# Moving the copies of x from ScalarE to VectorE in the first batch row of an attention and mixer kernel, and one load to another queue

## The chip, the cores and the metric

The kernel runs on one core of a Trainium2 chip. The metric is device time in microseconds (us), the median of a few executions. The core has four engines that compute: TensorE (PE; PEld is its weight load), VectorE (DVE), ScalarE (ACT) and GpSimd (POOL). SyncE (SP) only issues transfers, and ScalarE can issue them too. Each engine works through its own list of instructions in order. When the next instruction waits for data or for a free buffer, everything behind it on that engine waits as well, so the order of a list matters as much as its length.

## The reference

Eight batch rows of eight heads of thresholded attention are followed by a mixer: an MLP over tokens and an MLP over channels, both with a residual. Everything is float32.

```python
# q, k, v: (8, 8, 576, 64)
scores = scale * q @ k^T
thresh = max(scores, axis=-1) - tau
scores = where(scores >= thresh, scores, -1e9)
attn   = exp(scores - max(scores));  attn = attn / (sum(attn) + 1e-9)
x      = (attn @ v) laid out as (8, 576, 512)
# mixer
h   = relu(x^T @ w_tok1) @ w_tok2;   u = x + h^T
out = u + relu(u @ w_ch1) @ w_ch2
```

The four weight matrices arrive as 64-bit floats. The kernel converts them to 32-bit floats on the chip, in pieces, while it works.

## The kernel before

The work goes in units: 18 per batch row, 128 query rows of one pair of heads each (two of the 18 are shared by two pairs). Unit u has these stages: TensorE makes the scores; VectorE takes the row maxima (`mx`); ScalarE applies the threshold and the exponential (`e`, with row sums `rs`); VectorE inverts the sums (`rr`); GpSimd scales `e`. Two units later TensorE turns `e` (128x128 transposes into PSUM) and the turned blocks are copied to SBUF (`eT`). One unit after a group is complete TensorE multiplies it with the values (`pv` in PSUM), and that result is copied to SBUF as a part of `x` (kept transposed, `xT`). The turned blocks and `pv` share a pool of two PSUM buffers.

```python
ps_tr = ctx.enter_context(tc.tile_pool(name="ps_tr", bufs=2, space=bass.MemoryType.PSUM))
...
def scores(u):
    ...                                   # 8 or 16 matmuls into sc[0], sc[1]
    for h in range(2):
        nc.vector.tensor_reduce(out=mx[:, c], in_=sc[h][:, :, 0:HS], axis=AX.XY, op=ALU.max)
        nc.gpsimd.tensor_scalar(out=bias[:, c], in0=mx[:, c], ...)
def norm(u):
    nc.vector.tensor_scalar(out=rr, in0=rs, ...)
    nc.vector.reciprocal(out=rr, in_=rr)
    ...                                   # 2x nc.gpsimd.tensor_scalar: e times rr
def turn(u, third):
    ps = ps_tr.tile(...)                  # 3 transposes of 128x128 into ps
    on = nc.scalar.copy if third == 1 and u % 2 else nc.vector.tensor_copy
    on(out=eT[...], in_=ps)               # 128x384
def values(b, p, c):
    ps = ps_tr.tile(...)                  # 20 matmuls into ps
    ...
    nc.scalar.copy(out=x, in_=ps)         # 128x256, or 128x64 for a shared unit
```

From the second batch row on `e` is turned in another way: by a 32x32 transpose on VectorE and by transfers (`turn_blocks`).

A piece of weights is converted in three steps (k is the number of the step). `weight_to` issues steps up to a number, and each step gives work to several engines:

```python
def weight(n):
    for k in range(steps_done, ...):
        i, part = divmod(k, 3)
        if part == 0:
            on_gpsimd(i - 1)              # one add on GpSimd; then the raw buffer is free
            if i: load_piece(i - 1 + NRAW)
        else:
            on_scalar(i + 1, part - 1)    # ScalarE prepares the next piece
        on_vector(i, part)                # part 0: tensor_scalar; 1 and 2: scalar_tensor_tensor
```

The main loop, cut to what concerns the first batch row (`b_now` is 0 in units 0 to 17):

```python
for u in range(len(units) + LAG + 4):
    if on: scores(u)
    if due and not in_blocks(due[0][1]):
        values_due(u)                     # pv and its copy on ScalarE
    if 0 < u <= len(units): norm(u - 1)
    if b_now: weight(2)
    if back:
        for i in range(3): turn(w, i)     # w = u - 2, first batch row only
        ...
    if b_now: weight(2)
    else:     weight_to(2.25 * (u - 1.5)) # first step(s) of the unit
    if on: weigh(u)                       # threshold and exponential on ScalarE
    ...
    else:     weight_to(2.25 * (u - 1))   # second step(s) of the unit
    ...                                   # loads; prep(): VectorE transposes q and k of a pair
```

At the start the loads are issued in this order: q and k of pair 0 (on SP and ACT), weight piece 0 (SP), q and k of pair 1 (on SP and ACT), piece 1, v of pair 0, pieces 2 and 3, v of pair 1.

Of the kernel before, what the change touches and what calls it, by code (L numbers as in the profile page):

```python
# [21 lines left out]
def kernel(  # L22
# [26 lines left out]
    nc = tc.nc  # L49
# [47 lines left out]
    def load_qk(n, eng, part=None):  # L97


        b, p = pairs[n]  # L100
        if n not in loaded:
            loaded[n] = [ld.tile([P, S // 32, 32], F32, tag=tag, name=f"{tag}_{n}") for tag in ("lq", "lk")]
        for i in range(4) if part is None else (part,):
            h, c = divmod(i, 2)
            for src, t, on in zip((q, k), loaded[n], eng):
                on.dma_start(
                    out=t[32 * i : 32 * i + 32], in_=src[b, 2 * p + h, :, 32 * c : 32 * c + 32].rearrange("(n t) d -> t n d", t=32)
                )
# [29 lines left out]
    NRAW = 4  # L138
    raw_at = [scratch[:, 2 * WMAX * i : 2 * WMAX * (i + 1)] for i in range(NRAW)]

    def like(x, dst):
        if len(dst.shape) == 2:
            return x
        return x.rearrange("p (a b) -> p a b", a=dst.shape[1])
# [22 lines left out]
    def load_piece(i):  # L167
        if i >= len(pieces):
            return
        dst, src = pieces[i]  # L170
        rows = dst.shape[0]
        n = 1
        for d in dst.shape[1:]:
            n *= d
        raw = raw_at[i % NRAW][0:rows, 0 : n * (2 if wide(i) else 1)].bitcast(src.dtype)
        nc.sync.dma_start(out=like(raw, dst), in_=src)
        if wide(i):
            words = raw.bitcast(U32).rearrange("p (n w) -> p n w", w=2)
            h2 = work.tile([P, WMAX], F32, tag="o", name=f"h2_{i}")[0:rows, 0:n]
            raws[i] = like(words[:, :, 0], dst), like(words[:, :, 1], dst), like(h2, dst)  # L180
        else:
            raws[i] = like(raw, dst)

    def wide(i):
        return i < len(pieces) and pieces[i][1].dtype == I64

    def on_scalar(i, part):
        if wide(i):
            lo, hi, h2 = raws[i]
            if part == 0:  # L190
                nc.scalar.activation(out=lo.bitcast(I32), in_=lo, func=AF.Copy, scale=2.0**-29)
            else:
                nc.scalar.activation(out=h2, in_=hi.bitcast(F32), func=AF.Square)
# [17 lines left out]
    def on_gpsimd(i):  # L211
        if i >= 0:
            dst = pieces[i][0]
            if wide(i):
                nc.gpsimd.tensor_tensor(out=dst.bitcast(I32), in0=dst.bitcast(I32), in1=raws.pop(i)[0].bitcast(I32), op=ALU.add)
            else:
                nc.gpsimd.tensor_copy(out=dst, in_=raws.pop(i))
# [5 lines left out]
    def weight(n):  # L223

        nonlocal steps_done
        for k in range(steps_done, min(steps_done + n, 3 * len(pieces) + 1)):
            i, part = divmod(k, 3)
            if part == 0:
                on_gpsimd(i - 1)
                if i:  # L230
                    load_piece(i - 1 + NRAW)
            else:
                on_scalar(i + 1, part - 1)
            on_vector(i, part)
            steps_done = k + 1

    def weight_to(x):

        weight(max(int(x) - steps_done, 0))
# [3 lines left out]
        weight(3 * i + 4 - steps_done)  # L243

    load_piece(0)
    load_qk(1, (nc.sync, nc.scalar))
    load_piece(1)
    load_v(0)
    for i in range(2, NRAW):
        load_piece(i)  # L250
    load_v(1)

# [25 lines left out]
    def in_blocks(b):  # L278
        return b > 0
# [105 lines left out]
    def split_middle(n):  # L385
# [4 lines left out]
            nc.gpsimd.tensor_copy(out=vl[r, r], in_=lv[r, NI, :])  # L390
        vals[n] = lv, vl

    def values(b, p, c):

        lv, vl = vals[b * NP + p]
        if b not in xTs:
            xTs[b] = xTs[b + 1] = work.tile([P, NP, 2 * S], F32, tag="xT", name=f"xT_{b}")
        key = (b, p - p % 2, c) if c == "s" else (b, p, c)
        n, N, tok = (1, LAST, MAIN) if c == "s" else (2, 2 * P, 2 * P * c)
        first = LAST * (p % 2) if c == "s" else 0  # L400
        eT = eTs[key] if c == "s" else eTs.pop(key)
        if in_blocks(b):
            eT = eT[:, 0 : NK * n * P].rearrange("p (i c x) -> p c i x", i=4, c=NK)
            eT = eT[:, :, first // 32 : first // 32 + N // (32 * n), :]
        else:
            eT = eT[:, 0 : NK * n * P].rearrange("p (c x) -> p c x", c=NK)[:, :, first : first + N]
        ps = ps_tr.tile([P, MAIN], F32, tag="tr", name=f"pv_{b}_{p}_{c}")[:, 0:N]
        to = ps.rearrange("p (i x) -> p i x", x=32 * n) if in_blocks(b) else ps
        for h in range(2):
            r = slice(D * h, D * h + D)  # L410
            nc.tensor.matmul(to[r], lhsT=vl[:, r], rhs=eT[:, NI], start=True, stop=False, skip_group_check=True)  # L411
        for c in range(NI):
            for h in range(2):
                r = slice(D * h, D * h + D)
                j = (NI + 1) * h + c
                nc.tensor.matmul(to[r], lhsT=lv[:, j, :], rhs=eT[:, j], start=False, stop=(c == NI - 1), skip_group_check=True)  # L416
        x = xTs[b][:, p, S * (b % 2) + tok : S * (b % 2) + tok + N]
        if in_blocks(b) and n == 2:
            x = x.rearrange("p (n i x) -> p i n x", n=n, x=32)
            ps = ps.rearrange("p (i n x) -> p i n x", n=n, x=32)  # L420
        nc.scalar.copy(out=x, in_=ps)  # L421


    def token_mlp(b):
# [93 lines left out]
    def push(b):  # L518
        nonlocal quota
        uT = xTs[b]  # L520
        steps, old = token_mlp(b), list(todo)
        todo.clear()

        for i, step in enumerate(steps):
            n = 2 if i in (NT, NT + NTK) else 1
            todo.extend(old[:n] + [step])
            del old[:n]
        todo.extend(old)
        for i in range(2) if b % 2 == 0 else range(2, (2 * S + GR - 1) // GR):
            todo.extend(channel_mlp(b - b % 2, uT, i))  # L530
        quota = (sum(c for c, _ in todo) - (KEEP if b else KEEP_FIRST)) / (UB - 1)
# [6 lines left out]
    def values_due(u):  # L538
        while due and due[0][0] <= u:
            _, b, p, c = due.popleft()  # L540
            values(b, p, c)
            if p == NP - 1 and c == 1:
                push(b)

    for u in range(len(units) + LAG + 4):
        on = u < len(units)
        if u == UB:
            late.close()
            ps_mm = ctx.enter_context(tc.tile_pool(name="ps_mm", bufs=2, space=bass.MemoryType.PSUM))
        if on:  # L550
            b_now, p0, t = units[u]
            n = b_now * NP + p0
        w = u - LAG
        back = 0 <= w < len(units)
        if on:
            scores(u)

        if due and not in_blocks(due[0][1]):
            values_due(u)
        if 0 < u <= len(units):  # L560
            norm(u - 1)
        if b_now:
            weight(2)
        if back:
            key, place, many = group_of(w)
            if not in_blocks(key[0]):
                for i in range(3):
                    turn(w, i)
            if place == many - 1:
                b, p, c = key  # L570
                if c == 0 and p % 2 == 0:
                    split_middle(b * NP + p)
                if c == "s":
                    split_middle(b * NP + p + 1)
                when = u + (2 if in_blocks(b) else 1)
                due += [(when, b, p + i, c) for i in range(2 if c == "s" else 1)]
        if b_now:
            fill(0.4)
        if back and in_blocks(key[0]):
            turn_blocks(w)  # L580

        if b_now:
            weight(2)
        else:
            weight_to(2.25 * (u - 1.5))
        if on:
            weigh(u)
        elif b_now:
            fill(0.6)
        if b_now:  # L590
            weight(2)
        elif u == 0:
            on_scalar(0, 0)
            on_scalar(0, 1)
        else:
            weight_to(2.25 * (u - 1))
        if on:
            m = n + 2 + t // 4
            if t < 8 and m < len(pairs):
                load_qk(m, (nc.scalar if b_now else nc.sync,) * 2, t % 4)  # L600
                if t % 4 == 3:
                    load_v(m)
            if t == 2:
                prep(n + 1)
            if t == 7 and n + 2 < len(pairs):
                prep(n + 2)
        if due and in_blocks(due[0][1]):
            values_due(u)
# [31 lines left out]
```

## Time and profile before

| | |
|---|---|
| time, median of 3 | 1381.45 us (1379.32 to 1382.13) |
| span of the profiled execution | 1381.3 us |
| busy share of the span | PE 96%, DVE 43%, ACT 43%, POOL 26% |
| copies of x on ScalarE (all batch rows) | 64 of 128x256, 372 ns each |
| first batch row | about 12 to 106 us of the span |

In the views of the profile "busy" is the time in which an engine executed something; a bracket such as `[0.94 <-PE tr L360]` behind an instruction is the idle time just ahead of it on its engine, and what ended it. `L309` is line 309 of the kernel before: L286 are VectorE's transposes of q and k, L304 the score matmuls, L309 the maxima, L319 and L326 the threshold and exponential, L333 and L334 the inverse of the sums, L337 GpSimd's scaling, L360 the turns on TensorE, L362 the copies of turns, L411 and L416 the matmuls with the values, L421 the copies of x, and L201, L205 and L209 VectorE's three conversion steps (L191 and L193 ScalarE's, L215 GpSimd's).

### The profile page before, as it was taken

How to read it: one execution, taken by the hardware profiler on the slowest of the kernel's cores; microseconds unless marked ns; L12 is line 12 of the kernel's file. 1: busy time of each engine (PE TensorE's matmuls, PEld its weight loads, DVE VectorE, ACT ScalarE, POOL GpSimd, SP SyncE). 2: the span in 40 equal slices, each digit the busy share in tenths (PEclk: the TensorE clock that was granted, in tenths of full speed). 3: DMA queues.
4: the chain of work that ended last, by engine and by line, in shares of the span. 5: the costliest groups of instructions: out<-in, count | busy, mean ns of one | idle time of the engine just before them, and what ended most of it. 6: DMA issues, size and time to landing. Idle time of an engine off the chain costs nothing.

```text
span 1381.3 us, 19492 instructions
## 1 busy us (share of the span) xinstructions
PE 1330.3 (96%) x6866; PEld 834.1 (60%) x6866; DVE 590.3 (43%) x1009; ACT 589.5 (43%) x1328; POOL 354.8 (26%) x683
## 2 busy tenths in 40 slices
PE   6887789999999999999999999999999999999998
PEld 3544555646565666665766567565657566575675
DVE  5889875354444443434244444433343453201000
ACT  5776654445445444443434444353434454120110
POOL 3556653232323222222222222221221232100000
PEclk9988999999999999999999999999999999999999
DMA  5444654453444444433433444443333433300000
GB/s 118 109 105 120 180 150 119 109 129 89 110 121 105 98 110 101 105 81 88 109 87 93 104 95 107 99 102 81 94 90 92 110 74 88 83 8 16 8 8 23
DMA packets 257376, 128.34 MB, mean 93 GB/s; under 512 B 208064, under 2 KB 221376, under 8 KB 257280
## 3 DMA queue, kind: packets, MB, share of 16 engines
q1 hardware_dynamic: 129264, 111.16, 30.6%
q10 hardware_dynamic: 128016, 15.94, 7.3%
q8 instruction: 55, 0.90, 0.3%
q14 instruction: 41, 0.34, 0.1%
HBM read 43.25 MB, written 9.44 MB: 38 GB/s over the span
## 4 chain that ended last, share of the span: by engine, by line
PE 88%; DVE 6%; DMA 2%; SPq 1%; issue 1%; ACT 1%; POOL 1%; ACTq 0%; DVEq 0%; POOLq 0%
PE c L487 27%; PE c L471 27%; PE sc L304 11%; PE pv L416 8%; PE t L442 4%; PE t L449 4%; PE pv L411 3%; DVE mx L309 2%; PE c L483 1%; PE tx L433 1%; SPq L381 1%; PE pv_s L416 1%; DVE eT L362 1%; PE tr L360 1%; DMA eT<-T 1%
## 5 line engine op out<-in xcount | busy, mean ns | idle before, releaser
L309 DVE TENSOR_REDUCE mx<-sc 128x1 f32<-128x576 f32 x288 | 204.6, 751 | 488.6 <-PE sc L304 488.6
L471 PE MATMUL c<-xT,wc 128*128 128x256 f32 (+1 forms) x1920 | 401.0, 363 | 6.2 <-ACT g L472 5.0
L487 PE MATMUL c<-wc,g 128*128 128x512 f32 x864 | 390.7, 597 | 0.0
L471 PEld LDWEIGHTS c<-xT,wc 128*128 128x128 f32 x1920 | 335.0, 191 | 76.5 <-issue 29.0
L310 POOL TENSOR_SCALAR bias<-mx,toff 128x1 f32<-128x1 f32 x288 | 79.2, 275 | 803.1 <-DVE mx L309 746.5
L487 PEld LDWEIGHTS c<-wc,g 128*128 128x128 f32 x864 | 157.4, 190 | 175.6 <-issue 173.6
L319 ACT ACTIVATE e<-sc,bias 128x576 f32<-128x576 f32 x288 | 198.8, 739 | 141.4 <-POOL bias L310 141.2
L472 ACT ACTIVATE g<-c 128x256 f32<-128x256 f32 (+1 forms) x240 | 86.9, 362 | 328.8 <-PE c L471 315.4
L337 POOL TENSOR_SCALAR e<-e,rr 128x576 f32<-128x576 f32 x288 | 217.2, 767 | 16.8 <-DVE rr L334 4.7
L326 ACT ACTIVATE e<-e,ntau 128x576 f32<-128x576 f32 x288 | 220.8, 771 | 0.0
L304 PE MATMUL sc<-kT,qT 64*128 64x288 f32 (+1 forms) x1280 | 196.5, 441 | 15.0 <-DVE kT L286 9.7
L371 DVE STREAM_TRANSPOSE T<-e 128x1152 f32<-128x1152 f32 x126 | 172.6, 1370 | 13.3 <-DMA eT<-T 8.5
L304 PEld LDWEIGHTS sc<-kT,qT 64*128 64x128 f32 (+1 forms) x1280 | 107.3, 181 | 91.8 <-issue 44.8
L416 PE MATMUL pv<-eT,lv 128*64 128x256 f32 x1024 | 124.9, 386 | 0.0
L492 DVE COPY o<-c 128x512 f32<-128x512 f32 x36 | 24.9, 692 | 174.5 <-PE c L487 174.5
L416 PEld LDWEIGHTS pv<-eT,lv 128*64 128x64 f32 x1024 | 75.9, 140 | 39.0 <-issue 3.6
L421 ACT COPY xT<-pv 128x256 f32<-128x256 f32 x64 | 23.8, 372 | 174.8 <-PE pv L416 167.0
L449 PE MATMUL t<-w,a 128*128 128x288 f32 x256 | 75.2, 421 | 6.3 <-DVE xT L453 4.3
L442 PE MATMUL t<-x_sb,w 128*128 128x512 f32 x160 | 72.1, 597 | 0.0
L449 PEld LDWEIGHTS t<-w,a 128*128 128x128 f32 x256 | 46.0, 192 | 31.3 <-issue 11.5
L453 DVE TENSOR_TENSOR xT<-xT,t 128x288 f32<-128x288 f32 x64 | 28.2, 446 | 78.1 <-PE t L449 77.4
L326 ACT ACTIVATION_READ_ACCUMULATOR e<-e,ntau 128x1 f32 x288 | 56.6, 196 | 0.0
(48 smaller groups left out, 604.3 us busy)
## 6 DMA issues: line engine op xcount, KB each, us to landing
eT<-T SPq DMA_DIRECT2D x896, 72.0 KB, 2.0
scratch<-in_moe_w_ch_dram SPq DMA_DIRECT2D x24, 512.0 KB, 3.7
lv<-in_v_dram SPq DMA_DIRECT2D x32, 288.0 KB, 3.4
out_dram<-o SPq DMA_DIRECT2D x36, 256.0 KB, 2.1
lk<-in_k_dram ACTq DMA_DIRECT2D x112, 72.0 KB, 2.7
eT<-T SPq DMA_DIRECT2D x224, 36.0 KB, 1.9
lq<-in_q_dram ACTq DMA_DIRECT2D x104, 72.0 KB, 2.2
lq<-in_q_dram SPq DMA_DIRECT2D x24, 72.0 KB, 3.4
```

What stands on the lines that cost most here:

```text
L304: nc.tensor.matmul(sc[h][rows, f, 0:HS], lhsT=qT[r, cols], rhs=kT[r, HS * f : HS * f + HS], start=True, stop=True)
L309: nc.vector.tensor_reduce(out=mx[:, c], in_=sc[h][:, :, 0:HS], axis=AX.XY, op=ALU.max)
L319: nc.scalar.activation(out=eh, in_=sc[h][:, :, 0:HS], func=AF.Prelu, bias=bias[:, h : h + 1], scale=SCALE, alpha=STEEP)
L326: nc.scalar.activation(out=eh, in_=eh, func=AF.Exp, bias=ntau, accum_out=rs[:, h : h + 1])
L337: nc.gpsimd.tensor_scalar(out=eh, in0=eh, scalar1=rr[:, h : h + 1], scalar2=1.0, op0=ALU.mult, op1=ALU.mult)
L371: nc.vector.transpose(out=T.rearrange("p (a c n x) -> p c a n x", a=4, c=NK, n=n)[:, :, :, place, :], in_=e.rearrange("p (c a x) -> p c a ...
L416: nc.tensor.matmul(to[r], lhsT=lv[:, j, :], rhs=eT[:, j], start=False, stop=(c == NI - 1), skip_group_check=True)
L442: nc.tensor.matmul(ps, lhsT=w1[:, t, P * m : P * m + P], rhs=x_sb[:, t, :], start=(t == 0), stop=(t == NT - 1))
L449: nc.tensor.matmul(ps, lhsT=s["a"][:, m, P * c : P * c + P], rhs=w2[:, m, HS * f : HS * f + HS], start=(m == 0), stop=(m == NTK - 1))
L471: nc.tensor.matmul(ps, lhsT=wc1[:, j, c, :], rhs=uT[:, c, GR * i : GR * i + n], start=(c == 0), stop=(c == NCC - 1))
L472: nc.scalar.activation(out=s["g"][:, j, 0:n], in_=ps, func=AF.Relu)
L487: nc.tensor.matmul(flat, lhsT=s["g"][:, j, P * t : P * t + P], rhs=wc2[:, j, :], start=False, stop=(j == NJ - 1), skip_group_check=True)
```

## The change

In the first batch row the copies of `pv` into x go from ScalarE to VectorE. They are not issued where the matmuls are, but held back until after the maxima, the inverse of the sums and the first conversion steps of the unit; the copies of the turned blocks follow them. To have the first conversion steps there, `weight_to(2.25 * (u - 1.5))` moves from behind the turns to ahead of them. The step that hands a finished batch row to the mixer (`push`) waits for the held copies. At the start SP issues the keys of pair 1, which ScalarE issued before, and piece 1 of the weights comes after the values of pair 0. The change is meant to take ScalarE out of a wait for TensorE, and to give VectorE something to do while it waits for the turns. From the second batch row on, the copies of x stay on ScalarE.

```diff
     load_piece(0)
-    load_qk(1, (nc.sync, nc.scalar))
-    load_piece(1)
+    load_qk(1, (nc.sync, nc.sync))
     load_v(0)
-    for i in range(2, NRAW):
+    for i in range(1, NRAW):
         load_piece(i)
     load_v(1)
...
+    copies = deque()
     def values(b, p, c):
...
-        nc.scalar.copy(out=x, in_=ps)
+        if in_blocks(b):
+            nc.scalar.copy(out=x, in_=ps)
+        else:
+            copies.append(lambda: nc.vector.tensor_copy(out=x, in_=ps))
...
             if p == NP - 1 and c == 1:
+                if not in_blocks(b):
+                    return True
                 push(b)
+        return False
...
+        last = False
         if due and not in_blocks(due[0][1]):
-            values_due(u)
+            last = values_due(u)
         if 0 < u <= len(units):
             norm(u - 1)
         if b_now:
             weight(2)
+        else:
+            weight_to(2.25 * (u - 1.5))
+        while copies:
+            copies.popleft()()
+        if last:
+            push(0)
         if back:
...
         if b_now:
             weight(2)
-        else:
-            weight_to(2.25 * (u - 1.5))
         if on:
             weigh(u)
```

## The prediction

> **What bounds the kernel now.** I read the page first (busy shares, then the 40 slices), then the busy time by 20 us, then the waits and the engines' own timelines within the first batch row.
>
> ```profile
> PE 1330.3 (96%) x6866; PEld 834.1 (60%) x6866; DVE 590.3 (43%) x1009; ACT 589.5 (43%) x1328; POOL 354.8 (26%) x683
> ...
> PE   6887789999999999999999999999999999999998
> ...
> DVE  5889875354444443434244444433343453201000
> ```
>
> TensorE is the bound of the whole, but not in the first four or five slices of 34.5 us: there VectorE is at 8 to 9 tenths and TensorE at 6 to 8. The change touches only that stretch.
>
> ```profile
> 40.00:60.00 20.00, 17.03 (x144) 11.03 (x140) 17.04 (x38) 14.79 (x35) 12.02 (x22) 1.00 0.42 95
> 60.00:80.00 20.00, 16.80 (x110) 9.70 (x110) 15.91 (x35) 14.35 (x33) 10.90 (x21) 0.91 0.52 123
> 100.00:120.00 20.00, 12.30 (x63) 7.37 (x65) 18.38 (x32) 14.43 (x30) 13.06 (x16) 0.84 0.38 102
> 200.00:220.00 20.00, 20.00 (x76) 9.42 (x75) 11.10 (x18) 8.98 (x20) 8.08 (x16) 1.00 0.40 104
> ```
>
> Columns: stretch, its length, busy PE, PEld, DVE, ACT, POOL. Until about 160 us no engine is full; VectorE is closest (18.38 of 20 around 110 us). From 200 us on TensorE never stops, so whatever the early stretch gains or loses moves the end by the same amount.
>
> ```profile
> ACT xT L421 <- PE pv L416: 18.8, 8, 3.6
> PE tr L360 <- DVE eT L362: 14.8, 9, 5.3
> DVE eT L362 <- PE tr L360: 12.1, 20, 1.4
> ```
>
> These are waits from 20 to 145 us (total, times, longest). ScalarE waits 18.8 us for `pv`, which is what the change removes. But TensorE and VectorE wait for each other around the turns, and the chain of waits runs through those two (maxima, copies of turns, turns, scores, values); ScalarE's copies of x are hardly on it.
>
> ```profile
> 54.62 1.41 DVE L309 TENSOR_REDUCE mx<-sc 128x1 f32<-128x576 f32 x2
> 57.25 0.56 DVE L362 COPY eT<-tr 128x384 f32<-128x384 f32 x1 [0.94 <-PE tr L360]
> 58.45 0.56 DVE L362 COPY eT<-tr 128x384 f32<-128x384 f32 x1 [0.64 <-PE tr L360]
> 58.92 0.30 DVE L201 TENSOR_SCALAR w<-scratch 128x288 uint32<-128x288 uint32 x1
> 60.19 1.41 DVE L309 TENSOR_REDUCE mx<-sc 128x1 f32<-128x576 f32 x2
> 61.80 1.00 DVE L362 COPY eT<-tr 128x384 f32<-128x384 f32 x2
> 62.98 0.56 DVE L362 COPY eT<-tr 128x384 f32<-128x384 f32 x1 [0.18 <-PE tr L360]
> ```
>
> This is VectorE in units 9 and 10. In unit 9, which has a `pv`, it idles 0.94 us ahead of the first copy of a turn: a hole that the moved step and the copy can fill. In unit 10, without a `pv`, it idles 0.18 us only, and TensorE is the one that waits: its third turn starts at 62.39 us, 1.39 us late, for the copy begun at 61.80.
>
> **The skill.** The Trainium skill, "VectorE: DVE Perf Modes", section "The TRN2 errata", gives VectorE 120 cycles plus one per element at 0.96 GHz from PSUM: an estimate of 525 ns for 128x384, where the trace has 536 to 558, and so some 400 ns for 128x256. "SBUF — State Buffer", section "Who interferes with whom", says that a VectorE instruction with two SBUF inputs contends with GpSimd's reads, and that one with at most one SBUF input, outside the two-port modes, does not. The trace agrees: the L205 step on 128x288 takes 0.46 us at 59.25 but 0.95 at 63.79, beside GpSimd's add (63.51 to 64.42); the copies from PSUM keep their length. "DMA: Bandwidth & Descriptors", section "Issuing engines are not separate DMA queues", says that issuing from another engine saves only issue time; that fits what I expect of the load.
>
> **The change part by part.**
>
> *Copies.* Eight of 128x256 and four of 128x64 leave ScalarE (8 x 0.37 + 4 x 0.21 = 3.8 us). On VectorE I size them from two PSUM copies of this trace, 556 ns for 384 elements and 692 for 512, i.e. 1.06 ns per element and 0.15 fixed: 0.42 and 0.22 us, 8 x 0.42 + 4 x 0.22 = 4.2 us more on the busier engine. In units 9, 11, 13 and 15 `pv` ends about when the idle time begins or inside it (0.94, 0.60, 1.06 and 1.41 us), so the copy costs nothing, or 0.1 us in unit 11.
>
> *Moved steps.* One step per unit moves ahead of the copies of turns. In units 9, 11, 13 and 15 it fills the hole and leaves the path behind it: 0.30 + 0.45 + 0.42 + 0.68 = 1.85 us off. In units 8, 10, 12 and 14 it now stands between the maxima and the copy that TensorE waits for: 0.45 + 0.30 + 0.70 + 0.42 = 1.87 us on. That cancels. Worse, a step right behind `rr` meets GpSimd's scaling, which starts there; for the two-input steps of units 8 and 12 I add 0.25 us each, +0.5. In units 2, 3, 5 and 17 the step changes places with copies whose readers have slack: 0. In unit 4 VectorE idles 1.34 us ahead of the first copy, and the 0.68 us step goes in: -0.65.
>
> *Where the copy now waits for VectorE.* A PSUM buffer of `pv` comes free only with its copy, and VectorE has maxima first:
>
> ```profile
> 45.87 0.21 ACT L421 COPY xT<-pv_s 128x64 f32<-128x64 f32 x1 [0.28 <-PE pv_s L416]
> 46.45 0.21 ACT L421 COPY xT<-pv_s 128x64 f32<-128x64 f32 x1 [0.37 <-PE pv_s L416]
> ...
> 47.30 0.48 ACT L362 COPY eT<-tr 128x384 f32<-128x384 f32 x1 [0.64 <-PE tr L360]
> ```
> ```profile
> 45.19 1.42 DVE L309 TENSOR_REDUCE mx<-sc 128x1 f32<-128x576 f32 x2
> 46.52 0.16 DVE L333 TENSOR_SCALAR rr<-rs 128x2 f32<-128x2 f32 x1
> 46.72 0.17 DVE L334 RECIPROCAL rr<-rr 128x2 f32<-128x2 f32 x1
> 46.92 0.56 DVE L362 COPY eT<-tr 128x384 f32<-128x384 f32 x1
> ```
>
> In unit 7 both buffers hold a `pv`. ScalarE empties them at 46.1 and 46.7; VectorE cannot before `rr` (46.9) and the 0.45 us step, i.e. about 47.5 and 47.7, so the first turn starts more than 1 us later: +1.0 after the moved step is taken off again behind. In unit 6 ScalarE copies at 41.64 and VectorE could at 43.1: the second turn waits for it, +0.4. Unit 16 is like 7, but its `rr` is late anyway: +0.2.
>
> *Tail.* In units 18 and 20 VectorE is full: at unit 18 the copy adds its 0.42 less 0.1 of idle, +0.3. At unit 20 `pv` ends near 124.6, and VectorE reaches the copy after maxima, `rr` and two steps at 125.7; ScalarE had done it by 125.0. The transposes of x wait, partly made good since ScalarE's step is out of the way: +0.45.
>
> *Load.* Keys of pair 1 land long before they are used (24 to 25 us). The first path is pair 0's keys:
>
> ```profile
> 8.90 0.78 DVE L286 STREAM_TRANSPOSE kT<-lk 128x576 f32<-128x576 f32 x1 [2.41 <-DMA lk<-in_k_dram]
> ```
>
> They share the engines with piece 0 and pair 1 in either case; nothing now stands behind them in ScalarE's queue, for which I allow -0.3 us. The table load (9.25 us) moves ahead, but the first activation waits for maxima until 13.31: 0.
>
> Sum: +0.1 + 0 + 0.5 - 0.65 + 1.0 + 0.4 + 0.2 + 0.3 + 0.45 - 0.3 = +2.0 us. Unit shifts can be absorbed by slack that I did not see, so I take 1.5: 1381.45 + 1.5 = 1383.0 us.
>
> **Rivals.** First, ScalarE is freed and the path shortens. For it: 18.8 us of waits vanish. Against: in units 9, 11, 13 and 15 ScalarE's next instruction is a copy of a turn that comes after `pv` on TensorE anyway (56.78 and 57.79 in unit 9), so the exponential starts as late as before; only units 4, 16, 18 and 20 release it, by 0.7 to 1.4 us, where VectorE or TensorE is the one behind. If it did count in all eight waits, at some 0.5 us each, the time would be 1377. Second, VectorE is so full that copies and lengthened steps all land on the path: 4.2 us of copies plus about 1.5 us of contention, 1387. Third, the load: if pair 0's keys land up to 1 us sooner, everything behind moves by that.
>
> **Range and chances.** The terms are tenths of microseconds with both signs, and the runs of before spread over 2.8 us. The two full rivals give 1377 and 1387; I take 1378 to 1388 as eight in ten. Two per cent is 27.6 us, more than a quarter of the first batch row: a chance of 0.01 on either side, 0.98 for within.
>
> **What would show it.** Twelve VectorE copies xT<-pv near 0.4 and 0.2 us and none on ScalarE before the second row; ScalarE's 18.8 us wait gone, but mostly replaced by waits for turns; the idle time ahead of the first copy of a turn in units 9, 11, 13 and 15 filled; unit 7 longer by about 1 us; the third turn in even units waiting longer; kT of pair 0 within 1 us of 8.90. I am wrong if the units after 4 each become shorter, which would mean that ScalarE, or the hole, was worth more than I give it.

## The result, and the profile after

The changed kernel takes 1386.11 us (median of 6 runs, 1385.05 to 1388.32) against 1381.45 us (6 runs beside it, 1379.32 to 1383.14): a ratio of 1.0037, with a 95% interval of 1.0024 to 1.0050. It is a little slower. A second series of the same kernel gave 1.0025 [1.0011, 1.0039] (7 runs against 52). The profiled spans are 1383.5 us after and 1381.3 us before.

The page of the kernel after, its first two parts:

```profile
PE 1326.0 (96%) x6866; PEld 831.9 (60%) x6866; DVE 590.5 (43%) x1021; ACT 586.8 (42%) x1316; POOL 355.9 (26%) x683
...
PE   6876789999999999999999999999999999999998
...
DVE  5889874445444443434343444433333453101000
```

Twelve instructions have gone from ScalarE (1328 to 1316) to VectorE (1009 to 1021), and ScalarE has lost 2.7 us of work. VectorE's sum stays at 590 us all the same: it has 4.2 us more of copies, and its other instructions together took about as much less in this execution (the first conversion step on 128x512, for one, 13.1 us over the span in place of 15.5). Behind the fifth slice the digits differ by one tenth at most, in both directions.

The busy time of the kernel after in the same stretches as before (stretch, length, PE, PEld, DVE, ACT, POOL, each with its number of instructions; then granted clock, DMA share, GB/s):

```profile
40.00:60.00 20.00, 15.11 (x126) 9.44 (x123) 15.84 (x39) 11.07 (x25) 11.98 (x22) 0.91 0.42 94
60.00:80.00 20.00, 16.28 (x106) 9.82 (x106) 16.64 (x35) 15.21 (x32) 9.02 (x17) 0.91 0.52 124
100.00:120.00 20.00, 10.29 (x70) 6.23 (x69) 19.07 (x34) 13.21 (x26) 11.68 (x15) 0.91 0.43 110
200.00:220.00 20.00, 20.00 (x84) 9.95 (x83) 11.82 (x20) 8.99 (x20) 8.28 (x14) 1.00 0.46 116
```

From 40 to 60 us all of TensorE, VectorE and ScalarE do less than before in the same time (TensorE 15.11 against 17.03): the stretch is held up by waits, not by work. Around 110 us VectorE has come nearer to full (19.07 of 20, before 18.38). From 200 us on TensorE hardly stops (from 200 to 1340 us it is busy for 1136.07 us of 1140, in both traces), so a loss up to there reaches the end.

The waits of the kernel after from 20 to 145 us (who waits, for whom, total us, times, longest):

```profile
ACT eT L361 <- PE tr L359: 20.7, 8, 4.6
...
PE tr L359 <- DVE eT L361: 16.5, 9, 5.7
...
DVE eT L361 <- PE tr L359: 8.0, 17, 1.0
...
PE tr L359 <- DVE xT L426: 7.1, 5, 2.8
...
PE tx L438 <- DVE xT L426: 2.2, 1, 2.2
```

ScalarE's 18.8 us of waiting for `pv` is gone, and its wait for the turns has grown from 4.7 to 20.7 us in its place. VectorE waits less for turns (12.1 us before), but 3.0 us of waiting for `pv` are new. And TensorE, whose matmuls never waited for the copies of x before (only its weight loads did, 1.6 us in all), now waits 9.3 us for them on VectorE (units 6, 7, 15, 16, 18 and 20).

To see where the time goes I took the start of the first maxima of a unit, after less before. Only differences between two rows say what a stretch gained or lost.

| start of unit | after less before, us | what lies between |
|---|---|---|
| 0 | -1.33 | pair 0's keys were ready 1.34 us sooner in this execution |
| 4 | +0.43 | unit 3 longer, 3.4 to 5.3 us |
| 5 | -0.63 | unit 4 shorter, 7.0 to 6.0 us |
| 8 | +0.56 | units 6 and 7 longer, 4.0 to 4.6 and 5.4 to 6.1 us |
| 10 | +2.23 | units 8 and 9 longer, 4.1 to 4.6 and 5.6 to 6.7 us |
| 16 | +1.55 | units 10 to 15 |
| 18 | +1.82 | unit 16, 7.1 to 7.4 us |
| 22 | +2.13 | unit 20, 10.5 to 11.1 us, less 0.4 in unit 21; the spans end 2.2 apart |

A table like this has a trap, and unit 9 is it. TensorE on the timelines of after and of before, first `pv` of unit 9 after, then of unit 15 before:

```profile
56.47 2.83 PE L418 MATMUL pv<-eT,lv 128*64 128x256 f32 x16
```
```profile
87.08 3.12 PE L416 MATMUL pv<-eT,lv 128*64 128x256 f32 x16
```

The same sixteen matmuls take 1.90 us elsewhere. In both places the trace shows a granted clock of 0.50, after from 55 to 58 us and before from 87 to 89. So before a unit of two traces is compared, its matmuls have to be: of unit 9's 1.1 us, 0.93 is this. The Trainium skill, "TensorE: Matmul & The Clock Gate", section "What's actually happening", describes a gate that lets half of the clock pulses through when TensorE has been idle; the clock of 0.50 agrees, and TensorE had idled for 2.23 us shortly before, ahead of the third turn of unit 8 (1.83 before), which is less than the some 3.4 us that the page gives for an idle window. Two later traces with copies and steps in the same order have the slow stretch in unit 9 as well (2.68 and 2.78 us, behind the same wait of 2.23), so it may come with the change and not with the execution; no run separates the two. Over the whole stretch slow matmuls don't make the loss: between the first maxima of unit 0 and those of unit 22 TensorE was busy for 102.8 us after and 107.3 before, while the stretch took 134.0 and 130.5.

Unit 7 is the unit that was forecast to suffer most. VectorE and TensorE on the timeline of after (start, us, engine, line, operation, idle time ahead):

```profile
45.03 1.42 DVE L308 TENSOR_REDUCE mx<-sc 128x1 f32<-128x576 f32 x2 [0.17 <-PE sc L303]
46.37 0.16 DVE L332 TENSOR_SCALAR rr<-rs 128x2 f32<-128x2 f32 x1
...
46.65 0.44 DVE L209 SCALAR_TENSOR_TENSOR w<-h,w 128x288 f32<-128x288 f32 x1
47.00 0.35 DVE L426 COPY xT<-pv_s 128x64 f32<-128x64 f32 x2
47.27 0.87 PE L359 MATMUL tr<-ident,e 128*128 128x128 f32 x6 [1.02 <-DVE xT L426]
47.86 0.56 DVE L361 COPY eT<-tr 128x384 f32<-128x384 f32 x1 [0.51 <-PE tr L359]
```

Both PSUM buffers hold a finished `pv` from 46.3 us, TensorE stands still for 1.02 us, and then VectorE, which had just been the busy one, idles 0.51 us because the turns could not begin sooner. From `rr` to the first copy of a turn it is 1.49 us here and 0.40 before; 0.44 of that is the step.

### The profile page after: what moved, and what is told of

Its sections match the earlier page's. It is cut to its first block, busy times and chain, and to the rows that moved or that the text cites. A ratio compares the mean times of both kernels' runs of the same rounds, so it can differ in the third digit from the quotient of the medians.

```text
span 1383.5 us, 19492 instructions
## 1 busy us (share of the span) xinstructions
PE 1326.0 (96%) x6866; PEld 831.9 (60%) x6866; DVE 590.5 (43%) x1021; ACT 586.8 (42%) x1316; POOL 355.9 (26%) x683
## 4 chain that ended last, share of the span: by engine, by line
PE 88%; DVE 6%; ACT 2%; DMA 2%; SPq 1%; issue 1%; POOL 1%; DVEq 0%; ACTq 0%; POOLq 0%
PE c L492 27%; PE c L476 26%; PE sc L303 11%; PE pv L418 7%; PE t L447 5%; PE t L454 4%; PE pv L413 3%; DVE mx L308 2%; PE tx L438 1%; PE c L488 1%; SPq L380 1%; PE pv_s L418 1%; PE tr L359 1%; ACT e L318 1%; DVE eT L361 1%
## 5 line engine op out<-in xcount | busy, mean ns | idle before, releaser
L309 POOL TENSOR_SCALAR bias<-mx,toff 128x1 f32<-128x1 f32 x288 | 83.0, 288 | 806.5 <-DVE mx L308 749.8
L424 ACT COPY xT<-pv 128x256 f32<-128x256 f32 x56 | 20.8, 372 | 156.8 <-PE pv L418 149.5
```

## The experiments

What had to be told apart: is the loss that of the copies, of the moved steps, or of the load with what comes along with it? And if of the copies, of all twelve or of those that stand behind the maxima while both PSUM buffers are full? One more thing had turned up in the trace. Which of the two PSUM buffers a tile gets is decided when the program is built, and in the changed kernel the third turn of unit 3 got the buffer of the first turn, not of the second. It therefore waits for VectorE's copy. The timelines of TensorE, unit 3, after and before:

```profile
26.96 0.55 PE L359 MATMUL tr<-ident,e 128*128 128x128 f32 x3 [2.06 <-DVE eT L361]
```
```profile
26.27 0.55 PE L360 MATMUL tr<-ident,e 128*128 128x128 f32 x3 [0.57 <-ACT eT L362]
```

So some experiments write the buffer out by hand (called "pinned" here), as it was before: two tags of one buffer each, taken in turn by the turns, by `pv` and by the transposes of x, and kept for the third turn where the kernel before kept it.

```diff
+    side = [0]
+    def tr_tile(name, keep=False):
+        if not keep:
+            side[0] ^= 1
+        return ps_tr.tile([P, MAIN], F32, tag=f"tr{side[0]}", bufs=1, name=name)
...
-        ps = ps_tr.tile([P, MAIN], F32, tag="tr", ...)      # turns
+        ps = tr_tile(f"tr{third}_{u}", third == 2 and u in (1, 3, 15))
...
```

Every ratio below is to the kernel before on the same chip, with its 95% interval.

### Undoing one part at a time

**Without the load's change.**

```diff
-    load_qk(1, (nc.sync, nc.sync))
+    load_qk(1, (nc.sync, nc.scalar))
+    load_piece(1)
     load_v(0)
-    for i in range(1, NRAW):
+    for i in range(2, NRAW):
```

> The changed kernel without the load change; its third turn of unit 3 waits for ScalarE again. Theory (copies and steps alone are the loss; load and buffer cancel): within 1 us of the changed kernel, so 2.5 to 4.5 us slower than before. Rival (the load change is the loss): as fast as before.

1.0026 [1.0017, 1.0035], 1385.04 us (22 runs). The loss stays. Its third turn of unit 3 waits 0.57 us, for ScalarE, as before.

**The changed kernel, pinned.** Only the edit with the tags.

> The changed kernel with the buffers written out by hand: all as it has them but for unit 3, where the third turn takes the buffer of the second again, as in the kernel before. Theory (unit 3's lost 1.9 us are the buffer together with the step ahead of the first copy): 1.0 to 1.9 us faster than the changed kernel, so some 3 us slower than before; maxima of unit 4 near 28 us. Rival (unit 3's loss is made up in unit 4's idle time anyway): as slow as the changed kernel.

1.0025 [1.0016, 1.0033], 1384.84 us (21 runs). In this trace unit 3 has 3.9 us instead of 5.3, and units 3 and 4 together 9.7 (after 11.3, before 10.4). In the times that does not show: against the repeated series of the changed kernel there is no difference, against the first there is one of 0.0012, less than the intervals of the two together. Whether the changed buffer costs something stays open; it isn't the main loss.

**The changed kernel again**, unchanged, in a later series beside other kernels:

> The changed kernel once more, for a narrower interval: 1.0037 with 1.0024 to 1.0050 from six runs, where the run with unit 3's buffer put right gave 1.0025 (1.0016 to 1.0033) and the one without the load change 1.0026 (1.0017 to 1.0035). Theory (unit 3's buffer costs something beside the copies): 1.0032 or more. Rival (copies in the wrong units are all of it): 1.0025, as the two others.

1.0025 [1.0011, 1.0039], 1384.30 us (7 runs). It says how far two series of one kernel lie apart.

### Doing one part alone, from the kernel before

**The load alone, and the load alone with pinned buffers.** The edit is the load's part of the change.

> The kernel before with the load change alone (SP issues the keys of pair 1; piece 1 after the values of pair 0). In the changed kernel's trace pair 0's keys come 1.33 us sooner, but the third turn of unit 3 waits for VectorE's copy of the first turn, no longer for ScalarE's of the second: the program that builds the kernel gives it the other PSUM buffer once the loads stand in another order. Theory (the load is a gain, partly eaten by that buffer): 1.0 us faster than before, maxima of unit 0 at 10.7 us and of unit 4 near 28.6. Rival (the buffer costs more than the load brings): 0 to 1 us slower.

> The same with the buffers of the turns written out by hand as they were in the kernel before, so that only the load differs. Theory: the whole 1.3 us stays to the end, 1380.1 us where before is 1381.4. Rival (later slack absorbs it): no difference from before.

1.0006 [0.9994, 1.0018] (14 runs) and 1.0004 [0.9995, 1.0013] (21 runs; one more took 1554.75 us at a granted clock of 0.848 and is left out): nothing. The forecast gains of 1.0 and 1.3 us would be 0.9993 and 0.9991, outside both intervals. The earlier start of 1.33 us in the table is no effect of the load either. VectorE's first transpose of pair 0's keys, timelines of after, of steps_holes16_load (which has the load's change too) and of steps_holes16 (which hasn't):

```profile
7.56 0.78 DVE L285 STREAM_TRANSPOSE kT<-lk 128x576 f32<-128x576 f32 x1 [1.17 <-DMA lk<-in_k_dram]
```
```profile
9.60 0.78 DVE L285 STREAM_TRANSPOSE kT<-lk 128x576 f32<-128x576 f32 x1 [3.19 <-DMA lk<-in_k_dram]
```
```profile
7.04 0.78 DVE L286 STREAM_TRANSPOSE kT<-lk 128x576 f32<-128x576 f32 x1 [0.59 <-DMA lk<-in_k_dram]
```

Over fourteen traces that start lies between 6.81 and 9.60 us with the change (8 traces) and between 7.04 and 8.90 without (6): it varies from execution to execution, and one trace of each kernel can't show an effect of a few tenths.

**The steps alone.** `weight_to(2.25 * (u - 1.5))` ahead of the turns, copies and loads as before.

```diff
         if b_now:
             weight(2)
+        else:
+            weight_to(2.25 * (u - 1.5))
         if back:
...
-        else:
-            weight_to(2.25 * (u - 1.5))
```

> The kernel before with the first conversion steps of each unit moved ahead of the copies of turns, and nothing else (copies of x on ScalarE, loads as before; its waits for PSUM buffers are those of before). Copies and steps together cost some 3.5 us without the effect of unit 3's buffer. Theory (it is the copies that now wait behind the maxima; the steps cancel): within 1 us of before. Rival (the steps ahead of the copies that TensorE waits for are the loss): 2 to 3.5 us slower than before.

0.9988 [0.9980, 0.9996], 1380.39 us (22 runs against 73): about 1.6 us faster.

**The copies alone.** The twelve copies on VectorE, held back as in the change; steps behind the turns and loads as before.

> The kernel before with the copies of x of the first batch row on VectorE, behind maxima and the inverse of the sums and ahead of the copies of turns, and the steps and loads as before. Theory: 2.2 us slower than before, with most of it in units 6, 7, 16, 18 and 20, where a PSUM buffer stays full until VectorE has done its maxima. Rival (VectorE's list is simply 4.2 us longer): 4 us slower, spread over all units with a copy. Rival (the steps are the loss): no slower than before.

1.0021 [1.0012, 1.0029], 1385.02 us (22 runs): the copies are the loss. The time alone does not exclude the 4 us of the first rival (2.9 measured, 1.7 to 4.0 by the interval); the runs under "Which copies" do. And the two parts do not seem to add up: 1.0021 and 0.9988 would make 1.0009, while both together, in the run without the load, are 1.0026. The difference of 0.0017 is just over what the three intervals allow together (0.0015), and the third run stood on another chip, so the times alone do not settle it. Unit 16 shows it in the traces: 7.1 us before, 5.8 with the steps alone, 7.8 with the copies alone, 7.4 with both (6.7 in the pinned kernel, where unit 15 is 0.9 longer), while the two parts would add up to 6.5. And TensorE's matmuls wait 4.2 us for copies of x with the copies alone, and 9.3 to 9.4 in the three traces with both. The timelines say why. VectorE in unit 16 of after, of the kernel with the steps alone, and of the kernel before, from `rr` on:

```profile
96.90 0.17 DVE L332 TENSOR_SCALAR rr<-rs 128x2 f32<-128x2 f32 x1 [0.53 <-POOL bias L309]
...
97.19 0.67 DVE L205 SCALAR_TENSOR_TENSOR wc<-scratch,wc 128x512 uint32<-128x512 uint32 x1
97.78 0.35 DVE L426 COPY xT<-pv_s 128x64 f32<-128x64 f32 x2
98.63 1.02 DVE L361 COPY eT<-tr 128x384 f32<-128x384 f32 x2 [0.51 <-PE tr L359]
```
```profile
95.96 0.16 DVE L333 TENSOR_SCALAR rr<-rs 128x2 f32<-128x2 f32 x1
...
96.23 0.67 DVE L205 SCALAR_TENSOR_TENSOR wc<-scratch,wc 128x512 uint32<-128x512 uint32 x1
96.82 1.01 DVE L362 COPY eT<-tr 128x384 f32<-128x384 f32 x2
```
```profile
95.17 0.17 DVE L333 TENSOR_SCALAR rr<-rs 128x2 f32<-128x2 f32 x1 [0.16 <-ACT e L326]
...
96.05 1.02 DVE L362 COPY eT<-tr 128x384 f32<-128x384 f32 x2 [0.50 <-PE tr L360]
```

With the copies on ScalarE the turns run while VectorE does its step, and the copy of the turns follows without idle time: 0.86 us from `rr` to it, as in the kernel before (0.88, with 0.50 idle where the step now is). With the copies on VectorE the step stands ahead of the copies, the copies ahead of the turns, and the turns ahead of the next copy: 1.73 us from `rr` (96.90) to it, and 0.51 of that idle. The hole that the step was to fill has only moved behind it. Unit 6 shows the same on a small scale: 4.0 us before, 4.3 with either part alone, 4.6 with both.

### Which copies

**Copies on VectorE only where it idles.** From the pinned kernel: units 4, 9, 11, 13 and 15 keep their copies on VectorE, those of 6, 7, 16, 18 and 20 go back to ScalarE.

```diff
-        if in_blocks(b):
+        if in_blocks(b) or u not in (4, 9, 11, 13, 15):
             nc.scalar.copy(out=x, in_=ps)
```

> The changed kernel with unit 3's buffer put right, and with the copies of units 6, 7, 16, 18 and 20 back on ScalarE; VectorE keeps those of units 4, 9, 11, 13 and 15, where it idles. Theory (the five units make the loss): the 3.5 us of the run with unit 3's buffer put right shrink to 1.2 or less. Rival (it is the steps, or the copies in all units alike): 3 us or more stay.

0.9984 [0.9976, 0.9993], 1379.43 us (19 runs). With those seven copies back on ScalarE the loss is gone, and the kernel is some 2.2 us faster than the kernel before.

**The same with 18 and 20 on VectorE as well**, so that only units 6, 7 and 16 differ from the pinned kernel.

```diff
-        if in_blocks(b):
+        if in_blocks(b) or u in (6, 7, 16):
             nc.scalar.copy(out=x, in_=ps)
```

> As the run with copies in idle time only (0.9984), but the copies of units 18 and 20 are on VectorE too, as in the changed kernel; those of units 6, 7 and 16 stay on ScalarE. It splits the 5.7 us between that run and the one with all copies on VectorE. In the traces the PE waits for a VectorE copy of x are 1.3, 1.0 and 1.2 us in units 6, 7 and 16, and 2.9 and 2.2 in units 18 and 20. Theory (the waits of 18 and 20 lie mostly beside VectorE's own work; the maxima of unit 21 came 0.5 to 1 us late for unit 20): 1 to 2 us over the run with copies in idle time only, so 0.9991 to 0.9999. Rival (the longest waits cost most): 3.5 us or more over it, so 1.0010 or more.

0.9991 [0.9982, 1.0000], 1379.54 us (14 runs). From the pinned kernel to this one is 0.0034, with 0.0012 of uncertainty either way: 4.7 us, plus or minus 1.7, for the copies of three units. The pinned kernel ran in an earlier series; the changed kernel as it is, which ran beside this one, is 0.0034 above it too, with 0.0017 either way. From here to the one above, which ran on another chip, is 0.0007, plus or minus 0.0013: units 18 and 20 cost about 1 us, or nothing that these runs resolve. And the five copies in idle time cost nothing that these runs resolve either: 0.9984 with them, 0.9988 with the steps alone. One of them, unit 13 of after, on VectorE's timeline:

```profile
81.08 0.42 DVE L426 COPY xT<-pv 128x256 f32<-128x256 f32 x1 [0.38 <-PE pv L418]
81.55 0.56 DVE L361 COPY eT<-tr 128x384 f32<-128x384 f32 x1
```

VectorE reaches the copy before `pv` is done and takes it the moment it is; the turns are ready when it is through. Before, 1.06 us of idle time stood ahead of that copy of a turn.

By the lengths of units in the traces, the copies of units 6, 7 and 16 are worth some 0.2, 0.3 and 1.6 us (after against the steps alone: 4.55 and 4.31, 6.07 and 5.74, 7.39 and 5.82), 2.1 us in all. Such lengths repeat: unit 7 takes 6.1 us in all five traces that have its copies on VectorE, 5.6 to 5.7 in the three with the steps alone ahead there, 5.3 to 5.4 in the six others. But 2.1 is less than 4.7, and a little outside its uncertainty. What lies between the two I could not place. The traces of the pinned kernel and of this run lie 3.9 us apart between the first maxima of units 0 and 22 (134.0 and 130.1), and TensorE was busy for 2.3 us more in the first, so slower matmuls may be a part of it.

### Which steps

**Steps ahead only in five units**, where VectorE idled, from the kernel before:

```diff
+        elif u in (4, 9, 11, 13, 15):
+            weight_to(2.25 * (u - 1.5))
         if back:
```

The call behind the turns stays; it finds nothing left to do in these units.

> The kernel before with the first conversion steps ahead of the copies of turns in units 4, 9, 11, 13 and 15 only, where VectorE idles there for 0.6 to 1.4 us; copies of x on ScalarE, loads as before. Theory (a step in idle time leaves the path): 0.65 + 1.85 = 2.5 us faster than before. Rival (the next maxima wait for TensorE's scores, not for the steps, so that nothing is won): within 1 us of before.

0.9980 [0.9972, 0.9989], 1378.66 us (22 runs): 2.8 us off (1.5 to 3.9), against 2.5 expected.

**The same with unit 16**, since the steps alone had filled its hole:

> The kernel before with the first steps moved in units 4, 9, 11, 13 and 15, and in unit 16 as well, where the trace with steps alone had the next maxima 1.3 us sooner; copies and loads as before. Theory: another 0.5 to 1 us off the 0.998 of the run without unit 16, 0.9975 or less; faster than both kernels. Rival: 0.998 as without.

0.9977 [0.9970, 0.9983], 1378.23 us (20 runs against 52). This beats both kernels by its interval. From the five units to the six is 0.0003, which isn't resolved. Its waits from 20 to 145 us:

```profile
ACT xT L421 <- PE pv L416: 17.7, 8, 3.5
PE tr L360 <- DVE eT L362: 15.4, 10, 5.5
DVE eT L362 <- PE tr L360: 9.4, 18, 1.4
```

ScalarE waits 17.7 us for `pv`, nearly as long as in the kernel before, and the kernel is faster than either. What went down is VectorE's wait for turns, from 12.1 to 9.4. The wait that the change removes was worth nothing that these runs resolve; the idle time that it fills along the way was worth the 0.23%.

**The same with the load's change, pinned:**

> The same with the load change, and the buffers written out as they were. Pair 0's keys were turned at 6.8 to 8.9 us in five traces with the load change and at 8.2 to 8.9 in five without. Theory (the load brings some 0.8 us that stays): 0.0006 below the run without the load. Rival (it brings nothing at the end, as with the load alone): the same ratio.

0.9979 [0.9972, 0.9987], 1377.62 us (21 runs): the load adds nothing here either.

## Why the prediction was right, and where it was not

The direction was right, the size came out larger: the sum was +2.0 us, 1.5 were taken, and the medians lie 4.7 apart (by the interval of the ratio 3.3 to 6.9; the second series 1.5 to 5.4). That the sum came as near as it did is luck in part: the steps were put 1.5 us too high and the copies of units 6, 7 and 16 some 3 us too low, and the two errors partly cancel. The range of 1378 to 1388 us left room for a gain as well as for a loss. Point by point:

- **Sizes of the copies: right.** 0.42 and 0.22 us were worked out; the trace has 421 and 216 ns (eight and four instructions, spreads of 17 and 3 ns).
- **Odd units with a hole: right.** The idle time ahead of the first copy of a turn is filled in units 9, 11, 13 and 15, and the copies there cost nothing that the times resolve. Unit 15 is the weakest case: 1.41 us of idle time was read from an execution in which its sixteen matmuls took 3.12 us; with 1.90, in the trace of after, VectorE comes to the copy late, and TensorE waits 0.84 us for it.
- **Moved steps: the term was mis-sized.** The gains of 1.85 and 0.65 us in units 4, 9, 11, 13 and 15 came out in their sum: 2.5 forecast, 2.8 measured. But 1.87 us for the even units and 0.5 for GpSimd's share of SBUF were too much. In the trace of after the two-input steps of units 8 and 12, forecast to lengthen by 0.25 us each, take 0.44 and 0.67 us, where they took 0.45 and 0.75 before; what lengthens is GpSimd's small instruction beside them (`bias`, from 0.27 to 0.58 and 0.81 us). And TensorE's wait ahead of the third turn, which was to grow in the even units, grows in units 8 and 12 (1.83 to 2.23 and 1.59 to 2.31 us) and shrinks in 10 and 14 (1.39 to 1.25 and 2.03 to 1.87). In all, the steps were to cancel (-0.1 us); alone they gave 1.6 us (interval 0.5 to 2.8). The traces have no rise in all even units; which of them has the slack was not measured.
- **Copies of units 6, 7 and 16: the term that failed.** +0.4, +1.0 and +0.2, 1.6 us in all; the runs show 4.7 plus or minus 1.7, the lengths of the units in the traces 2.1. The mechanism was as described, two full PSUM buffers that are emptied only behind maxima, `rr` and a step. Unit 16 was the worst misjudged. "Its `rr` is late anyway" was true, but ScalarE had emptied the buffers at 95.2 and 95.8, so the turns were on their way while VectorE waited for `rr`; with the copy behind `rr` and the step, everything starts after it. And I sized copies and steps as separate terms, where each makes the other worse.
- **Tail, units 18 and 20: +0.75 was forecast,** 0.0007 measured, about 1 us and not resolved. TensorE's wait of 2.2 us ahead of the transposes of x in unit 20 is there, but unit 20 is only 0.5 us longer, and 21 is 0.4 shorter.
- **Load: -0.3 was forecast, nothing was found.** Three comparisons: load alone, load alone pinned, and on the fastest kernel. The keys of pair 0 start within 1.34 us of the time before, not within 1, and that is scatter.
- **Unit 3, put at 0:** "copies whose readers have slack" did not reckon with the changed buffer, which made the third turn wait for VectorE's copy of the first, 2.06 us of wait in the trace. Part of it came back in unit 4, and the times can't resolve the rest.
- **Rivals.** That ScalarE was on the path (1377 us) is refuted: its wait vanished and the kernel got slower. That VectorE is so full that every copy counts (1387 us) comes near in time but for the wrong reason: five copies out of twelve are free. The Trainium skill, "Perfetto Trace Analysis", section "Optimizing Scalar/DVE Operations", says that it may make sense to move work from VectorE to ScalarE where VectorE is saturated. The change goes the other way, and the runs agree with the advice only in part: around 50 us VectorE is busy 16 to 17 of 20 us, and what decides is not that share but what stands ahead of the copy in its list.

## What to carry to other kernels

Give the emptying of a PSUM buffer to the engine that can reach it when the result is done, not to the one with the fewest waits: a wait at the end of which the engine's next work would have to wait as well is worth nothing, and a copy behind long instructions holds up the engine that needs the buffer. Fill the idle time of the nearly full engine with work that nobody waits for (here six conversion steps, 0.23%), and only in those units where the idle time is seen ahead of an instruction. Two changes that use the same hole need not add up, so measure each alone and both together, and look at whether a reordering has changed which buffer a tile gets.

## What was not expected of the hardware

The kernel before, 67 runs in the first series of experiments, lay between 1376.35 and 1385.92 us; the runs with a mean granted TensorE clock of 0.993 or more lay between 1376.35 and 1380.76, those with 0.986 between 1381.35 and 1384.96. The clock is not all of it: 23 runs at 0.990 lay between 1379.24 and 1385.92. That is more than the effect in question, so only medians of some twenty runs could tell the parts apart. Within a trace sixteen equal matmuls took 1.90 us or up to 3.12 (3.63 in one of the experiments), where the granted clock fell to 0.50. And the first keys, loaded at the start in the same order by the same queue, were there for VectorE's transpose at anything from 6.8 to 9.6 us.
